# Two MLPs behind a linear attention on one core: the first batch's queries projected once and woven among the keys

## The chip, the cores and the metric

The kernel runs on one core of one Trainium2 chip. The metric is the time of one execution on the device in microseconds (us). The core has a matrix engine (TensorE, in the profile PE, with its weight loads as PEld), VectorE (DVE), ScalarE (ACT), GpSimd (POOL), and SyncE (SP), which here only issues transfers. Transfers are issued by SP, ACT and POOL, each in its own order.

## The reference

Random-feature attention on 4 batches of 8 heads with 576 tokens and 64 columns per head, then two MLPs on the 2304 tokens:

```python
def phi(x):
    proj = np.einsum('bhsd,df->bhsf', x, w_phi)               # 128 features
    proj = proj - np.max(np.abs(proj), axis=-1, keepdims=True)
    return np.concatenate([np.exp(proj), np.exp(-proj)], axis=-1)
q_p, k_p = phi(q), phi(k)
kv  = np.einsum('bhsf,bhsd->bhfd', k_p, v)
z   = np.sum(k_p, axis=2)
num = np.einsum('bhsf,bhfd->bhsd', q_p, kv)
den = np.einsum('bhsf,bhf->bhs', q_p, z)[..., None] + 1e-06
x   = (num / den).transpose(0, 2, 1, 3).reshape(2304, 512)
h = x @ w_in;   x = np.maximum(0.01 * h, h) @ w_out           # 512 -> 2048 -> 512
g = x @ w_gate; out = (g * (1 / (1 + np.exp(-g))) * (x @ w_val)) @ w_out2   # 512 -> 1536 -> 512
```

The subtracted maximum is one number per token and head; for a query it makes the same factor in `num` and `den`, apart from the 1e-06.

## The kernel before

Heads go in pairs (j = 0 to 3), because two heads of 64 columns fill the 128 partitions. Tokens go in five blocks of 96 or 128 for the keys and in two halves of 288 (t = 0, 1) for the queries. Batches are done one after another. While TensorE works on the MLPs of one batch, the attention of the next lies between their steps. Only the first batch has nothing to lie beside: its attention is the start of the program, and the change is there.

**First batch, keys.** `first_k` projects two blocks (L446, two heads of 128 features at once), takes the largest absolute value per token and head (L459), subtracts it (L60) and makes both exponentials on ACT (L464, L465). `first_back` multiplies them with the values, beside which stand columns of ones for `z` (L220), and `k_z` copies the sum of all blocks to SBUF (`kvh`).

**First batch, queries.** `first_q` projects the queries of two blocks with tokens on partitions, only to take the maxima (L473). `q_m` turns these maxima and spreads them over 18 groups of 32 tokens with a mask (L330, L333, L335). `q_exp` then projects the queries a second time, now with features on partitions (L393), and adds the negative maxima by a second matmul with `sel` into the same PSUM bank (L394); ACT makes the exponentials (L396, L397). `q_num` multiplies with `kvh` (L414), `q_fin` turns the denominators, inverts, turns them back and multiplies (L422 to L432), and splits the result in a high and a low part, `xh` (ACT, L63) and `xl` (DVE, L60). The MLP's matmuls take these as their moving side.

The later batches have another way for the queries: `q_p` projects them once with features on partitions, and a reduction that turns as it goes (L352) takes maxima over 32 partitions out of PSUM; `q_m_t` turns what is left on TensorE (L364), ends the maximum (L369) and spreads it (L372 to L377). `q_exp` adds the `sel` matmul to the projection that is still in its bank.

`pm` and `pa` are two pools of four PSUM banks each. `first_k`, the query projections and the MLP products use `pm`, `q_num` and the key sums use `pa` (`bk`).

**Weights.** They arrive as 64-bit numbers; `w_to_f32` makes them 32-bit (ACT L595, L596, L599; DVE L600 or L604 and L605, L610) and `w_split` splits them in high and low parts (L620, L60). Some results are stored (`kept`, `parts`) and read back by later batches. In the first attention, `early` converts the first four gate weights and stores them; they are read back before the gate's first unit.

**What sets the order.** `first_steps` makes a list of steps: in each come the next key block pair, the products of the pair two steps back, and the query maxima of the pair four steps back; sixteen steps of `q_exp` and, two behind, `q_num` and `q_fin` follow. The tile framework then puts the instructions of each engine in an order by a model of their times and priorities; within that order every engine waits for its operands by semaphores. The rows of that order below are from the built programs.

Of the kernel before, what the change touches and what calls it, by code (L numbers as in the profile page):

```python
# [17 lines left out]
P = 128  # L18
B, H, S, D = 4, 8, 576, 64
F = 128  # L20
# [12 lines left out]
NC = TOPS + P + 18 + NB  # L33
# [9 lines left out]
def linear_attention_two_mlps(ctx: ExitStack, tc, qT, kT, vt, w_phi, w1, w2, wg, wv, w3, cst, out):  # L43
# [25 lines left out]
    mask = cst_sb[:, TOPS + P : TOPS + P + 18]  # L69
    mask_t = cst_sb[:, TOPS + P + 18 : NC]  # L70
    sel = const.tile([P, 4, P], F32R, name="sel")
# [6 lines left out]
    mm = [const.tile([P, 32], F32R, name=f"mm{i}") for i in range(4)]  # L78
# [3 lines left out]
    def load_constants():  # L82
        signs.append(T([P, 4, P], F32, "es", 5))
# [41 lines left out]
    def lean(b):  # L125

        return b >= 1
# [198 lines left out]
    def q_m(b, j):  # L326
        n = 2 * NST
        m = mq.pop((b, j))
        t = mm[j % 2]
        dve.tensor_copy(t[:, 0:n], m)  # L330
        sub(t[:, n : 2 * n], m, t[:, 0:n].bitcast(F32))
        mt = T([P, 32], F32, "mt", 1)
        dve.transpose(out=mt, in_=t.bitcast(F32))  # L333
        r = mrow[b, j] = T([P, 18, 32], F32R, "acc", 4)
        dve.tensor_tensor(  # L335
            out=r,
            in0=mt.rearrange("p (o i) -> p o i", o=1).to_broadcast([P, 18, 32]),
            in1=mask.rearrange("p (k o) -> p k o", o=1).to_broadcast([P, 18, 32]),
            op=ALU.mult,
        )  # L340

    def q_p(b, j, t):
# [18 lines left out]
    def q_m_t(b, j, t):  # L361
# [8 lines left out]
        x = mm[2 + t]  # L370
# [3 lines left out]
        if t == 0:  # L374
            mrow[b, j] = T([P, 2 * NB, 32], F32R, "mrow", 1)
# [4 lines left out]
            in1=mask_t.rearrange("p (k o) -> p k o", o=1).to_broadcast([P, NB, 32]),  # L380
# [3 lines left out]
    def q_exp(b, j, h, t):  # L384
        if lean(b):
            ps = pt.pop((b, j, h, t))[:, 0:HT]
            r = mrow[b, j][:, NB * t : NB * t + NB].rearrange("p k i -> p (k i)")
            pe.matmul(ps, sel[:, 2 + h], r, start=False, stop=True, skip_group_check=True)  # L388
        else:
            ps = bk(b)[:, 0:HT]  # L390
            c = slice(HT * t, HT * t + HT)
            r = mrow[b, j].rearrange("p k i -> p (k i)")[:, c]
            pe.matmul(ps, wbd[:, h], raw["q", b, j][:, c], start=True, stop=False)  # L393
            pe.matmul(ps, sel[:, h], r, start=False, stop=True)  # L394
        f = T([P, 2, HT], F32, "ff" if lean(b) else ("ff", "fh", "fl")[(2 * t + h + j) % 3], 3)
# [46 lines left out]
    def project(kind, j, s, n):  # L442
        ps = bk(0)
        for i in range(n):
# [3 lines left out]
                raw[kind, 0, j][:, o],  # L448
# [5 lines left out]
        return ps[:, 0 : 2 * F * n].rearrange("p (r f) -> p r f", f=F)  # L454

    def first_k(j, s, n):
        pv = project("k", j, s, n)
# [11 lines left out]
    def first_q(j, s, n):  # L469
        pv = project("q", j, s, n)  # L470
        if s == 0:
            mq[0, j] = T([P, 2 * NST], F32, "mq", 2)
        dve.tensor_reduce(  # L473
            out=mq[0, j][:, 2 * s : 2 * s + 2 * n], in_=pv, axis=AX.X, op=ALU.max, apply_absolute_value=True
        )
        if s + n == NST:
            q_m(0, j)

# [6 lines left out]
    def first_steps():  # L485

        n, lag = len(pairs), 4
        steps = [[] for _ in range(n + lag)]
# [4 lines left out]
        groups = [(j, t, h) for j in range(NP) for t in range(2) for h in range(2)]  # L493
        for i in range(len(groups) + 2):
            todo = []
            if i < len(groups):
                j, t, h = groups[i]
                todo.append(lambda j=j, t=t, h=h: q_exp(0, j, h, t))
            if i >= 2:
                j, t, h = groups[i - 2]  # L500
                todo.append(lambda j=j, t=t, h=h: q_num(0, j, h, t))
                if h == 1:
                    todo.append(lambda j=j, t=t: q_fin(0, j, t))
            steps.append(todo)
# [169 lines left out]

    def early(key):

        w_load(key, "gp", 5)
        w_to_f32(key)
        del wf[key]

# [421 lines left out]

    def splits(i):
        for k in slots[i]:
            ahead(loaded, w_load, done[0] + 2)
            ahead(conv, w_to_f32, done[0] + 2)
# [133 lines left out]
```

## Time and profile before

| | |
|---|---|
| Time, median of three runs | 1075.07 us (1073.3 to 1075.19) |
| Profiled execution | 1074.16 us, span 1072.3 us |
| TensorE busy | 1050.2 us, 98% of the span |
| DVE busy | 793.6 us, 74% |
| ACT busy | 651.0 us, 61% |
| Transfers | 237.37 MB, mean 221 GB/s |

Busy time is the time in which an engine has at least one instruction running; matmuls overlap each other, so a row's mean time is more than its place in the sequence costs. In the profile a matmul of 32-bit numbers appears as two pieces. The shares are means over stages that differ: the first batch's attention, the MLPs of batches 0 to 2 with the next batch's attention between, and the last batch.

### The profile page before, as it was taken

Reading aid. Unit: us, or ns where it says so; the run is one execution under the profiler, and the core shown is the slowest. Engines: PE = TensorE matmul, PEld = TensorE weight load, DVE = VectorE, ACT = ScalarE, POOL = GpSimd, SP = SyncE. Lnnn points to the kernel's source line nnn. Section 1 sums busy time; section 2 is a strip of 40 time slices with the busy share of each in tenths; the row PEclk is TensorE's granted clock in tenths of the full one; section 3 lists DMA queues with packets and bytes.
Section 4 is the critical chain, followed back from the end, with each engine's and each line's share of the span. In section 5 each row is a group of like instructions: output and inputs, shape, how many; then the busy total and the mean of one; then the engine's idle time right before and its main releaser. Section 6 shows DMA issues by size and latency. Waiting matters only on the chain.

```text
span 1072.3 us, 20451 instructions
## 1 busy us (share of the span) xinstructions
PE 1050.2 (98%) x7670; PEld 1025.1 (96%) x7670; DVE 793.6 (74%) x1712; ACT 651.0 (61%) x1443; POOL 21.9 (2%) x57
## 2 busy tenths in 40 slices
PE   9989999999999999999999989999999999999998
PEld 8869999999999999999999989999999999999998
DVE  5987788888889978879685855958879632468473
ACT  4878887789868787656553466745444334336542
POOL 1000100000000000000000000000000000000000
PEclk9999999999999999999999999999999999999999
DMA  9536767557665995686553386436977767658542
GB/s 301 172 101 221 247 197 264 189 194 236 213 217 187 332 356 195 258 335 225 180 184 131 120 331 224 176 126 235 326 261 263 275 216 276 203 176 293 192 144 84
DMA packets 101922, 237.37 MB, mean 221 GB/s; under 512 B 19904, under 2 KB 35648, under 8 KB 101824
## 3 DMA queue, kind: packets, MB, share of 16 engines
q1 hardware_dynamic: 95136, 220.73, 59.6%
q0 software_dynamic: 4032, 14.68, 3.6%
q8 instruction: 61, 1.00, 0.4%
q10 hardware_dynamic: 2656, 0.66, 0.3%
q14 instruction: 37, 0.30, 0.1%
HBM read 170.49 MB, written 65.54 MB: 220 GB/s over the span
## 4 chain that ended last, share of the span: by engine, by line
PE 64%; DMA 5%; ACT 2%; DVE 2%; issue 0%; SPq 0%; DVEq 0%; ACTq 0%
PE pm L691 44%; PE pa L817 9%; PE pm L817 5%; PE pa L414 2%; PE pa L232 2%; DMA wr<-kept 1%; PE pa L179 1%; DMA wi<-parts 1%; DMA parts<-wi 1%; DMA wi<-in_wv_dram 1%; DMA sums<-wr 1%; DMA vhl<-parts 0%; PE pa L388 0%; PE pa L350 0%; DVE xl L60 0%
## 5 line engine op out<-in xcount | busy, mean ns | idle before, releaser
L691 PE MATMUL pm<-xh,wi 128*128 128x288 f32 x1664 | 352.7, 298 | 2.1 <-ACT xh L63 0.9
L691 PE MATMUL pm<-gp,wo 128*128 128x288 f32 x2256 | 339.0, 296 | 2.6 <-ACT acc L63 1.3
L691 PEld LDWEIGHTS pm<-gp,wo 128*128 128x128 f32 x2256 | 312.0, 188 | 4.9 <-ACT gp L63 2.0
L691 PEld LDWEIGHTS pm<-xh,wi 128*128 128x128 f32 x1664 | 272.2, 188 | 6.0 <-ACT xh L63 1.7
L691 PE MATMUL pm<-xl,wi 128*128 128x288 f32 x832 | 246.5, 297 | 0.5 <-DVE xl L60 0.5
L691 PEld LDWEIGHTS pm<-xl,wi 128*128 128x128 f32 x832 | 156.3, 188 | 1.6 <-DVE xl L60 1.2
L758 DVE TENSOR_TENSOR acc<-pm,acc 128x288 f32<-128x288 f32 x160 | 70.1, 452 | 43.9 <-PE pm L691 43.3
L60 DVE TENSOR_TENSOR gp<-es,gp 128x576 fp32r<-128x576 f32 x94 | 70.5, 750 | 28.5 <-ACT gp L63 28.0
L63 ACT ACTIVATE gp<-es 128x576 fp32r<-128x576 f32 x94 | 64.4, 687 | 28.7 <-DVE es L739 23.4
L60 DVE TENSOR_TENSOR wi<-wr,wi 128x512 fp32r<-128x512 f32 x96 | 65.2, 684 | 20.6 <-ACT wi L620 19.8
L620 ACT ACTIVATE wi<-wr 128x512 fp32r<-128x512 f32 x96 | 59.8, 634 | 29.0 <-PE pm L691 8.2
L817 PE MATMUL pm<-xh,wi 128*128 128x288 f32 x272 | 62.6, 296 | 2.4 <-DMA wi<-parts 1.5
L60 DVE TENSOR_TENSOR fl<-ff,fh 128x512 fp32r<-128x512 f32 (+1 forms) x72 | 51.2, 713 | 9.2 <-ACT fh L63 8.8
L596 ACT ACTIVATE wi<-wi 128x512 int32<-128x512 uint32 x64 | 43.6, 682 | 23.5 <-DMA wi<-in_w_dram 16.5
L595 ACT ACTIVATE wr<-wi 128x512 f32<-128x512 f32 x64 | 43.8, 684 | 10.9 <-DMA wi<-in_w_dram 6.8
L817 PEld LDWEIGHTS pm<-xh,wi 128*128 128x128 f32 x272 | 46.4, 188 | 3.6 <-DVE es L863 2.0
L610 DVE TENSOR_TENSOR wr<-wr,wi 128x512 uint16<-128x512 uint16 x64 | 48.1, 752 | 0.9
L63 ACT ACTIVATE fh<-ff 128x512 fp32r<-128x512 f32 (+1 forms) x72 | 47.3, 663 | 1.0
L417 ACT ACTIVATE dn<-pa 64x288 f32<-64x288 f32 x64 | 26.1, 407 | 30.1 <-PE pa L414 29.2
L719 ACT ACTIVATE es<-pm 128x288 f32<-128x288 f32 x72 | 29.3, 420 | 22.3 <-PE pm L817 17.1
L63 ACT ACTIVATE acc<-pm 128x288 f32<-128x288 f32 x64 | 26.3, 424 | 26.0 <-PE pm L691 25.9
L739 DVE SCALAR_TENSOR_TENSOR es<-pm,es 128x288 f32<-128x288 f32 x72 | 32.1, 449 | 12.6 <-PE pm L691 12.3
(217 smaller groups left out, 2086.8 us busy)
## 6 DMA issues: line engine op xcount, KB each, us to landing
wo<-parts SPq DMA_DIRECT2D x77, 512.0 KB, 6.1
wi<-parts SPq DMA_DIRECT2D x68, 512.0 KB, 6.0
parts<-wi SPq DMA_DIRECT2D x56, 512.0 KB, 4.6
wi<-in_w_dram SPq DMA_DIRECT2D x44, 512.0 KB, 4.6
wr<-kept SPq DMA_DIRECT2D x68, 256.0 KB, 4.4
parts<-wo POOLq DMA_DIRECT2D x28, 512.0 KB, 5.6
kept<-wr SPq DMA_DIRECT2D x40, 256.0 KB, 4.3
wi<-in_wv_dram SPq DMA_DIRECT2D x12, 512.0 KB, 4.1
```

The source lines that it names most:

```text
L60: dve.tensor_tensor(out=o, in0=a, in1=b, op=ALU.subtract)
L63: act.activation(o, a, AF.Copy)
L417: act.activation(dn[b, j, t][D * h : D * h + D], ps[D:P], AF.Copy, bias=1e-6)
L595: act.activation(t, high.bitcast(F32), AF.Abs, scale=REBIAS)
L596: act.activation(low, low.bitcast(U32), AF.Copy, scale=2.0**-29)
L610: dve.tensor_tensor(out=t16, in0=t16, in1=e16, op=ALU.add)
L620: i = act.activation(t[:, 0], r, AF.Copy)
L691: m = pe.matmul(ps, w, x[:, c], start=(i == 0), stop=(i == n - 1))
L719: act.activation(o, i, AF.Prelu, alpha=0.01)
L739: dve.scalar_tensor_tensor(out=g[:, c], in0=ps, scalar=0.5, in1=g[:, c], op0=ALU.mult, op1=ALU.mult)
L758: dve.tensor_tensor(out=acc[o][:, t], in0=ps, in1=acc[o][:, t], op=ALU.add)
L817: m = pe.matmul(ps, a, b, start=start and n == 0, stop=stop and n == 5, skip_group_check=True)
```

## The change

The queries of the first batch go the way of the later batches: one projection with features on partitions, here in plain 32-bit (`wbd`), maxima turned from PSUM, `sel` added in the same bank. `first_q`, `q_m` and the constants for them are gone. `first_steps` now gives every call a time and sorts by it, so that the queries of a pair stand among the keys of the next. The early conversions of four gate weights are gone; those weights are converted in their turn like the others. The warm-up has five matmuls for three. `wbd` is loaded from ACT's queue, and the first keys come in two transfers. The splits of the first four weights are no longer called in one step but in four.

```diff
-        for i in range(3):
+        for i in range(5):
             pe.matmul(ps[:, 0 : 2 * F], zero[:, 0:F], zero, start=True, stop=True)
...
-        nc.sync.dma_start(out=t, in_=kT[b, j])
-        if not (b or j):
-            nc.sync.dma_start(out=wbd.rearrange("p h f -> p (h f)"), in_=w_phi)
+        if b or j:
+            nc.sync.dma_start(out=t, in_=kT[b, j])
+        else:
+            nc.scalar.dma_start(out=wbd.rearrange("p h f -> p (h f)"), in_=w_phi)
+            for c in (slice(0, 256), slice(256, S)):
+                nc.sync.dma_start(out=t[:, c], in_=kT[b, j][:, c])
...
-            a = qs[b, j][h][:, c]
-            pe.matmul(ps, wst_h, a, start=True, stop=False)
-            pe.matmul(ps, wst_l, a, start=False, stop=True)
+            if b == 0:
+                pe.matmul(ps, wbd[:, h], raw["q", b, j][:, c], start=True, stop=True)
+            else:
+                a = qs[b, j][h][:, c]
+                pe.matmul(ps, wst_h, a, start=True, stop=False)
+                pe.matmul(ps, wst_l, a, start=False, stop=True)
...
-        if lean(b):
-            ps = pt.pop((b, j, h, t))[:, 0:HT]
-            r = mrow[b, j][:, NB * t : NB * t + NB].rearrange("p k i -> p (k i)")
-            pe.matmul(ps, sel[:, 2 + h], r, start=False, stop=True, skip_group_check=True)
-        else:
-            ps = bk(b)[:, 0:HT]
-            c = slice(HT * t, HT * t + HT)
-            r = mrow[b, j].rearrange("p k i -> p (k i)")[:, c]
-            pe.matmul(ps, wbd[:, h], raw["q", b, j][:, c], start=True, stop=False)
-            pe.matmul(ps, sel[:, h], r, start=False, stop=True)
+        ps = pt.pop((b, j, h, t))[:, 0:HT]
+        r = mrow[b, j][:, NB * t : NB * t + NB].rearrange("p k i -> p (k i)")
+        pe.matmul(ps, sel[:, h], r, start=False, stop=True, skip_group_check=True)
...
-        for i, p in enumerate(pairs):
-            steps[i].append(lambda p=p: first_k(*p))
-            steps[i + 2].append(lambda p=p: first_back(*p))
-            steps[i + lag].append(lambda p=p: first_q(*p))
...
+        for i, (j, s, n) in enumerate(pairs):
+            at(i, first_k, j, s, n)
+            at(i + 2.5, first_back, j, s, n)
+        for g in range(2 * NP):
+            j, t = divmod(g, 2)
+            base = 3 + 1.25 * g
+            last = max(base + 2.4, 3 * j + 4.6 + 0.4 * t)
+            at(base + 0.1, q_p, 0, j, t)
+            at(base + 0.9, q_m_t, 0, j, t)
+            for h in range(2):
+                at(base + 1.5 + 0.2 * h, q_exp, 0, j, h, t)
+                at(last + 0.2 * h, q_num, 0, j, h, t)
+            at(last + 0.25, q_fin, 0, j, t)
...
-    pre, made, start = 4, 0, 8
     for i, todo in enumerate(steps):
...
-            splits(-1)
-        if i == 14:
+        if i in (6, 8, 10, 12):
+            split_next()
+        if i == 13:
             split_constants()
             load_k(1, 0)
-        while made < pre * min(1, max(0, (i + 1 - start) / (len(steps) - start))):
-            with tc.high_priority(offset=-300):
-                early(("g", 0, made))
-            made += 1
```

In the rows of order a name is a tile with its number, result first, then operands; a line number belongs to its own kernel. TensorE at the start of the program: `pm` are the PSUM banks of the projections, `raw_87` the keys of the first pair, `pk_110` (before) and `pk_111` (now) its queries. In the kernel before:

```order
L109 MATMUL pm_83<-es_81 128x256 x3
L446 MATMUL pm_141<-wbd,raw_87 128x256 x2
L446 MATMUL pm_150<-wbd,raw_87 128x256 x2
L446 MATMUL pm_168<-wbd,raw_87 128x256
L446 MATMUL pm_184<-wbd,raw_99 128x256 x2
L446 MATMUL pm_193<-wbd,pk_110 128x256 x2
L220 MATMUL pa_159<-xh_90,wo_146 128x128 x8
L446 MATMUL pm_204<-wbd,raw_99 128x256 x2
```

The same place on TensorE in the changed kernel:

```order
L108 MATMUL pm_81<-es_79 128x256 x5
L424 MATMUL pm_142<-wbd,raw_87 128x256 x2
L424 MATMUL pm_151<-wbd,raw_87 128x256 x2
L424 MATMUL pm_160<-wbd,raw_87 128x256
L424 MATMUL pm_181<-wbd,raw_100 128x256 x2
L332 MATMUL pm_190<-pk_111,wbd 128x288
L218 MATMUL pa_168<-xh_91,wo_147 128x128 x8
L332 MATMUL pm_193<-pk_111,wbd 128x288
```

The block projections of the queries (`pm_193<-wbd,pk_110`, 256 columns) are gone, and the 288-column projections that stood in `q_exp` (L393) have come to the front, between the keys (L332).

DVE at the first pair's query maxima (`mq`, now `cst_sb` and `top`) up to the spread maxima `acc` that the `sel` matmul takes. In the kernel before:

```order
L473 TENSOR_REDUCE mq_196<-pm_310 128x2
L330 CAST mm_77<-mq_196 128x10
L60 TENSOR_TENSOR mm_77<-mq_196,mm_77 128x10
L333 STREAM_TRANSPOSE mt_315<-mm_77 128x32
L335 TENSOR_TENSOR acc_317<-mt_315,cst_sb 128x576
L604 TENSOR_SCALAR wr_246<-wr_246 128x512
```

The same place on DVE in the changed kernel:

```order
L354 TENSOR_REDUCE top_205<-pm_193 18x32
L337 TENSOR_REDUCE cst_sb<-pm_220 128x9
L357 CAST mm_77<-top_205 18x32
L337 TENSOR_REDUCE cst_sb<-pm_223 128x9
L60 TENSOR_TENSOR mm_77<-top_205,mm_77 18x32
L362 TENSOR_TENSOR acc_209<-mm_77,cst_sb 128x288
L354 TENSOR_REDUCE top_249<-pm_223 18x32
L357 CAST mm_78<-top_249 18x32
L60 TENSOR_TENSOR mm_78<-top_249,mm_78 18x32
L362 TENSOR_TENSOR acc_209<-mm_78,cst_sb 128x288
L572 TENSOR_SCALAR wr_355<-wr_355 128x512
```

Where one chain of five rows ended in one product of 576 columns, two chains, one per half, lie in each other, with two further maxima (`pm_220`, `pm_223`) between them, and each `top` waits for a turn on TensorE.

TensorE at the end of the attention, where the last numerators (`pa`) meet the first MLP matmuls (`wi`). In the kernel before:

```order
L691 MATMUL pm_823<-xl_643,wi_262 128x288
L691 MATMUL pm_823<-xh_642,wi_262 128x288
L691 MATMUL pm_892<-xl_643,wi_281 128x288
L691 MATMUL pm_892<-xh_642,wi_281 128x288
L414 MATMUL pa_760<-ff_725,kvh_480 128x288 x2
L414 MATMUL pa_771<-fh_736,kvh_480 128x288 x2
L691 MATMUL pm_809<-xh_708,wi_262 128x288
```

The same place on TensorE in the changed kernel, up to the first MLP matmuls:

```order
L349 MATMUL pm_641<-cst_sb 128x128
L372 MATMUL pm_561<-acc_618,sel 128x288
L372 MATMUL pm_564<-acc_618,sel 128x288
L392 MATMUL pa_702<-ff_656,kvh_700 128x288 x2
L652 MATMUL pm_764<-xh_287,wi_371 128x288
L652 MATMUL pm_764<-xl_288,wi_371 128x288
L652 MATMUL pm_764<-xh_287,wi_371 128x288
L652 MATMUL pm_764<-xh_443,wi_371 128x288
```

Before, the last four numerator groups and those ahead of them stood between the MLP's matmuls of the third pair; now the first MLP matmul (`pm_764<-xh_287`) stands behind nearly all of the attention, and only the last pair's work is between the units.

## Rows read from the trace of the kernel before

**Rows 1.** Stretches: length, busy us (instructions) PE, PEld, DVE, ACT, POOL, clock, DMA.
```profile
7.26:22.80 15.54, 15.54 (x100) 14.32 (x100) 10.69 (x26) 9.00 (x18) 0.00 (x0) 1.00 1.10 347
22.80:50.00 27.20, 26.44 (x162) 22.97 (x161) 25.92 (x60) 19.95 (x41) 0.96 (x3) 1.00 0.61 202
...
22.80:84.45 61.65, 55.71 (x292) 45.02 (x290) 54.06 (x126) 45.55 (x103) 2.26 (x6) 1.00 0.44 145
...
170.00:220.00 50.00, 48.95 (x361) 47.82 (x360) 42.24 (x85) 33.78 (x66) 2.22 (x4) 1.00 0.59 191
220.00:310.00 90.00, 86.39 (x601) 81.76 (x600) 81.09 (x172) 80.79 (x164) 4.27 (x8) 1.00 0.70 232
```

**Rows 2.** Timeline (start us, length us, instruction, idle before): DVE's maxima; the last wait.
```profile
22.05 0.76 DVE L335 TENSOR_TENSOR acc<-mt,cst_sb 128x576 fp32r<-128x576 f32 x1
...
84.00 0.45 DVE L60 TENSOR_TENSOR xl<-xf,xh 128x288 fp32r<-128x288 f32 x1
...
84.51 0.40 PE L691 MATMUL pm<-xl,wi 128*128 128x288 f32 x1 [0.37 <-DVE xl L60]
```

**Rows 3.** Timeline of TensorE: warm-up, keys, values, numerators.
```profile
1.10 2.93 PE L109 MATMUL pm<-es 128*128 128x256 f32 x6 [1.10 <-POOL es L106]
...
5.18 6.00 PE L446 MATMUL pm<-wbd,raw 128*128 128x256 f32 x14 [1.15 <-DMA wbd<-in_w_phi_dram]
...
20.73 1.95 PE L220 MATMUL pa<-xh,wo 96*128 96x128 f32 x16
...
25.14 2.75 PE L446 MATMUL pm<-wbd,pk 128*128 128x256 f32 x12
...
50.62 1.13 PE L414 MATMUL pa<-fl,kvh 128*128 128x288 f32 x4
...
52.20 1.13 PE L414 MATMUL pa<-ff,kvh 128*128 128x288 f32 x4
```

**Rows 4.** Groups on DVE, 0 to 100 us: shapes, count, busy us, mean ns, idle before.
```profile
L473 DVE TENSOR_REDUCE mq<-pm 128x4 f32<-128x512 f32 x8 | 5.5, 684 | 0.9 <-PE pm L446 0.9
...
L335 DVE TENSOR_TENSOR acc<-mt,cst_sb 128x576 fp32r<-128x576 f32 x4 | 3.0, 755 | 0.1
L610 DVE TENSOR_TENSOR wr<-wr,gp 128x512 uint16<-128x512 uint16 x4 | 3.0, 743 | 0.1
L600 DVE SCALAR_TENSOR_TENSOR wr<-wr,gp 128x512 int32<-128x512 int32 x4 | 2.8, 693 | 2.6 <-ACT gp L599 2.6
...
L473 DVE TENSOR_REDUCE mq<-pm 128x2 f32<-128x256 f32 x4 | 1.7, 424 | 2.5 <-PE pm L446 2.5
...
L333 DVE STREAM_TRANSPOSE mt<-mm 128x32 f32<-128x32 f32 x4 | 0.8, 208 | 0.1
```

**Rows 5.** Groups on DVE over the whole span: the later batches' query maxima.
```profile
L352 DVE TRANSPOSE_TENSOR_REDUCE cst_sb<-pa 128x9 f32<-128x288 f32 x48 | 22.0, 471 | 5.3 <-PE pa L351 5.2
...
L377 DVE TENSOR_TENSOR mrow<-mm,cst_sb 128x288 fp32r<-128x288 f32 x24 | 10.7, 447 | 0.3
...
L369 DVE TENSOR_REDUCE top<-pa 18x32 f32<-18x128 f32 x24 | 6.5, 270 | 1.6 <-PE pa L364 1.5
...
L372 DVE CAST mm<-top 18x32 fp32r<-18x32 f32 x24 | 3.7, 156 | 0.2
```

**Rows 6.** Groups on ACT, 0 to 100 us: the early conversions.
```profile
L595 ACT ACTIVATE wr<-gp 128x512 f32<-128x512 f32 x4 | 2.8, 701 | 0.0
L599 ACT ACTIVATE gp<-gp 128x512 int32<-128x512 f32 x4 | 2.7, 675 | 0.0
...
L596 ACT ACTIVATE gp<-gp 128x512 int32<-128x512 uint32 x4 | 2.4, 657 | 0.0
```

**Rows 7.** Groups on TensorE over the whole span: the later batches' turn.
```profile
L364 PE MATMUL pa<-cst_sb 128*128 128x128 f32 x24 | 6.6, 274 | 0.5 <-DVE cst_sb L352 0.5
```

**Rows 8.** The chain that ended last: start us, length us, what.
```profile
307.70 8.60 PE pm L691 x65
```

**Rows 9.** The turning maxima of L352: what they waited for (us, times).
```profile
  PE pa L351: 5.2, 5
```

More of the change, by code (lines that the diff above doesn't have):

```diff
@@ L32 @@
 TOPS = 4 * NB
-NC = TOPS + P + 18 + NB
+NC = TOPS + P + NB
 OFF = (0, 128, 256, 352, 448)
@@ L68, in linear_attention_two_mlps @@
     ident = cst_sb[:, TOPS : TOPS + P]
-    mask = cst_sb[:, TOPS + P : TOPS + P + 18]
-    mask_t = cst_sb[:, TOPS + P + 18 : NC]
-    sel = const.tile([P, 4, P], F32R, name="sel")
+    mask = cst_sb[:, TOPS + P : NC]
+    sel = const.tile([P, 2, P], F32R, name="sel")
     ones = const.tile([P, P], F32R, name="ones")
@@ L77, in linear_attention_two_mlps @@
     wbd_l = const.tile([P, 2, F], F32R, name="wbd_l")
-    mm = [const.tile([P, 32], F32R, name=f"mm{i}") for i in range(4)]
+    mm = [const.tile([P, 32], F32R, name=f"mm{i}") for i in range(2)]
     signs = []
     def load_constants():
-        signs.append(T([P, 4, P], F32, "es", 5))
+        signs.append(T([P, 2, P], F32, "es", 5))
         nc.sync.dma_start(out=cst_sb, in_=cst[:, 0:NC])
@@ L324, in q_split @@
         sub(s1[0:D], r[D:P], s1[D:P].bitcast(F32))
[L326 to L340, printed above, removed]
     def q_p(b, j, t):
@@ L369, in q_m_t @@
         dve.tensor_reduce(out=top, in_=turned.rearrange("r (g i) -> r i g", g=4), axis=AX.X, op=ALU.max)
-        x = mm[2 + t]
+        x = mm[t]
         hi = x[0 : 2 * NB]
@@ L379, in q_m_t @@
             in0=x.bitcast(F32).rearrange("p (o i) -> p o i", o=1).to_broadcast([P, NB, 32]),
-            in1=mask_t.rearrange("p (k o) -> p k o", o=1).to_broadcast([P, NB, 32]),
+            in1=mask.rearrange("p (k o) -> p k o", o=1).to_broadcast([P, NB, 32]),
             op=ALU.mult,
@@ L447, in project @@
                 ps[:, 2 * F * i : 2 * F * i + 2 * F],
-                raw[kind, 0, j][:, o],
+                raw["k", 0, j][:, o],
                 wbd.rearrange("p h f -> p (h f)"),
@@ L467, in first_k @@
             ff[0, j, s + i] = f[:, i]
[L469 to L477, printed above, removed]
     def first_back(j, s, n):
@@ L485, in first_steps, with at @@
     def first_steps():
-        n, lag = len(pairs), 4
-        steps = [[] for _ in range(n + lag)]
-        for i, p in enumerate(pairs):
-            steps[i].append(lambda p=p: first_k(*p))
-            steps[i + 2].append(lambda p=p: first_back(*p))
-            steps[i + lag].append(lambda p=p: first_q(*p))
[L493 to L504, printed above, removed]
+        events = []
+        def at(time, fn, *args):
+            events.append((time, len(events), lambda: fn(*args)))
+        for i, (j, s, n) in enumerate(pairs):
[11 more added lines that the diff above has]
+            at(last + 0.25, q_fin, 0, j, t)
+        steps = [[] for _ in range(int(max(e[0] for e in events)) + 1)]
+        for time, _, fn in sorted(events, key=lambda e: e[:2]):
+            steps[int(time)].append(fn)
         return steps
@@ L673, in w_sums @@
             nc.sync.dma_start(out=d, in_=t)
[L675 to L679, printed above, removed]
     gp, acc, x2h, x2l, sg = ({} for _ in range(5))
@@ L1101, in depth, with split_next @@
         return 4 if any(k[1] == 1 for k in nxt) else 5
+    def split_next():
+        ahead(loaded, w_load, done[0] + 2)
+        ahead(conv, w_to_f32, done[0] + 2)
+        ahead(done, w_split, done[0] + 1)
+        keep_all_but(2 if done[0] < len(order) and order[done[0]][1] < 2 else 0)
+        ahead(loaded, w_load, done[0] + depth())
     def splits(i):
         for k in slots[i]:
-            ahead(loaded, w_load, done[0] + 2)
-            ahead(conv, w_to_f32, done[0] + 2)
-            ahead(done, w_split, done[0] + 1)
-            keep_all_but(2 if done[0] < len(order) and order[done[0]][1] < 2 else 0)
-            ahead(loaded, w_load, done[0] + depth())
+            split_next()
     atts = {}
@@ L1144, in linear_attention_two_mlps @@
             fn()
-        if i == 4:
+        if i == 2:
             query_constants()
@@ L1172, in _constants @@
     import numpy as np
-    c = np.zeros((P, NC + 4 * P), np.float32)
+    c = np.zeros((P, NC + 2 * P), np.float32)
     c[:, TOPS : TOPS + P] = np.eye(P)
-    signs = c[:, NC:].reshape(P, 4, P)
-    blocks = [(s, a) for s in range(NST) for a in range(VAL[s] // 32)]
-    for p in range(P):
-        a, r = divmod(p, 32)
-        if r >= 4 * NST:
-            continue
-        st, h = divmod(r % (2 * NST), 2)
-        signs[p, h] = -1.0
-        for k, (s2, a2) in enumerate(blocks):
-            c[p, TOPS + P + k] = float(s2 == st and a2 == a)
+    signs = c[:, NC:].reshape(P, 2, P)
     for part in (0, 32):
@@ L1188, in _constants @@
             for k in range(NB):
-                c[part + NB * h + k, TOPS + P + 18 + k] = 1.0
-                signs[part + NB * h + k, 2 + h] = -1.0
+                c[part + NB * h + k, TOPS + P + k] = 1.0
+                signs[part + NB * h + k, h] = -1.0
     return c
```

13 lines of the change are left out of this document (5 added, 8 removed).

## The prediction

> **What bounds the kernel now.** I read the stretches first [rows 1]. From 88 us on TensorE hardly stops: even in the weakest later stretch, 220 to 310 us, it is busy 86.39 of 90. The change leaves the sum of that later work alone, so a gain has to come from the time before the first MLP block runs without stops. There DVE carries the load. In 22.80 to 84.45 us it is busy 54.06 of 61.65 us, and in the part to 50 us 25.92 of 27.20 (95%); what is left, 50 to 84.45, has 28.14 of 34.45 (82%). The reader should see in the waits why the end of this stretch is set by DVE [rows 2]: the last row of TensorE that still waits is a matmul at 84.51 us, for the low half `xl` that DVE (L60) starts at 84.00 and ends at 84.45. So the measure of the change is how much earlier that `xl` comes (last pair, first half of the tokens). The profiled execution took 1074.16 us, 1.86 more than its span and 0.9 below the median of the three runs; the sum is made against 1074.16.
>
> **The start.** The warm-up's six pieces end at 4.03 us, TensorE then waits 1.15 us for `wbd`, and fourteen key pieces take 6.00 us, 0.43 each; the same pieces take 2.75/12 = 0.229 at 25 us [rows 3]. [...] Ten pieces at 0.43 to 0.49 last from 1.10 to about 5.7 us and start the last at about 5.0, so that rest is filled. `wbd` now goes first on ACT's queue, ahead of six value loads that each move back by one place, and the first key columns come as a smaller transfer on SP's. Fourteen pieces at 0.229 save 2.8 us of TensorE. DVE idles 4.85 of the 15.54 us up to 22.80, where the first query maxima are spread out (L335 starts at 22.05 and lasts 0.76) [rows 1, 2]; no more than that can go, and if the warm-up itself holds up the first key matmul, 0.5 us is lost. Between -0.5 and 4.85 I take 2 us, near the 2.8, because the new chain for the first maxima has two trips to TensorE in it. That point then lies at 20.8 us.
> [...]
>
> **Queries on DVE.** Removed: eight maxima of 0.684 and four of 0.424 us (7.2), and four times the old spreading (L335 0.755, the turn 0.208, two small casts priced at 0.156 each: 5.1) [rows 4, 5]. Added: sixteen turning maxima of 0.471 (7.5) and eight times 0.270 + 0.156 + 0.156 + 0.447 (8.2); the last three forms are those that later batches use, and the subtraction is priced as the cast [rows 5]. Net, DVE gets 3.4 us more. Each of the eight groups also gains a trip: DVE's maxima, a turn on TensorE, DVE again, then the `sel` matmul; before, only DVE's result was waited for.
>
> **No early conversions.** In this stretch DVE loses four shifts of 0.693 and four additions of 0.743 us: 5.7 [rows 4]. ACT loses four times 0.701 + 0.675 + 0.657 = 8.1 us [rows 6]. So DVE's work behind the start changes by 15.7 - 12.3 - 5.7 = -2.3, from 54.06 to 51.8 us.
>
> **Queries on TensorE.** Twenty projections of two pieces go: 40 x 0.229 = 9.2 us [rows 3]. The sixteen 288-column projections are not new, they stood in `q_exp` and move forward. Added are eight turns, of 0.274 us at most: 2.2 [rows 7]. The attention's own matmuls then are keys 9.2, values 160 pieces x 1.95/16 = 19.5, sixteen groups of projection, `sel` and two numerator matmuls at 52.20 - 50.62 = 1.58 (25.3; both [rows 3]), turns 2.2: 56.2 us. With 42 MLP matmuls of 8.60/65 = 0.132 ahead of the last `xl` (5.5) [rows 8], and a start at 5.2, TensorE alone could be done at 66.9 us. It is not the bound; its 7 us saved count only as far as DVE waits less for it.
>
> **Interleaving.** Before, keys and query maxima came first and the sixteen numerator groups last, where DVE had only the long chain of transposes and products plus conversions, and stood still 6.3 us in 50 to 84.45. Now these chains lie among key work of later pairs. How busy DVE will be is the main unknown: no lower than 54.06/61.65 = 88% if the trips cost what the chain gives back, no higher than 100%. The nearest rows are the mixed stretch to 50 us (95%) and 220 to 310 (81.09/90 = 90%) [rows 1]; I take 93%. Then 51.8/0.93 = 55.7 us, and the `xl` ends at 20.8 + 55.7 = 76.5 us: 7.95 us earlier than 84.45. What TensorE does behind it is the same in both: the two other halves are covered by units that are ready.
>
> **Given back.** The four gate weights are now converted with those of the value matrix, in about 175 to 225 us, where before they were read back ready. In 170 to 220 TensorE loses 1.05 of 50 us (2%), in 220 to 310, where gate and value weights are both converted, 3.61 of 90 (4%) [rows 1]. Two per cent more of 55 us is 1.1 us; ACT there is busy 33.78 of 50, which is the cover. Without it the price is up to ACT's 8.1 us; nothing is the other end, and a gain is excluded, since work is only added. I take 1.2. SP loses four loads of 512 KB and four stores in front of the first batch's next loads, and four reads back; its transfers are not what the first stretch waits for, so they count nothing, up to the start term's own bound.
>
> **Sum.** 1074.16 - 7.95 + 1.2 = 1067.4 us. At 88% (58.9 us, end 79.7) it is 1070.6, at 100% (51.8, end 72.6) 1063.5; with a start 2 us to either side the own range is 1062 to 1072.
>
> **Rivals.** (1) *TensorE and DVE both stay fed.* For: 95% in the first mixed stretch. With DVE at 100% and a start 4.85 us earlier, the end is 17.95 + 51.8 = 69.8, still above TensorE's 66.9; take 71.5. Against: the numerators wait for PSUM that DVE empties. Time 1074.16 - 12.95 + 0.6 = 1061.8, at best 1060.
> (2) *The conversions cost their full price.* ACT's 8.1 us come back later, where the gain has to be paid out: 1074.16 - 7.95 + 8.1 = 1074.3, no change. For: DVE and ACT are at 90% in 220 to 310 us. Against: 16 of 50 us free on ACT in the stretch before.
> (3) *The turned maxima stall DVE: slower.* DVE takes its queue in order, and behind each of the two maxima of a group stand conversions, key maxima and the other chain's transposes. In later batches five of these maxima waited for their projection for 5.2 us together [rows 9]. If all sixteen trips (eight to the projection, eight to the turn) wait 1.04 us, DVE idles 16.6 us, and the end is 20.8 + 51.8 + 16.6 = 89.2: 1074.16 + 4.75 + 1.2 = 1080.1. It decides from 10.6 us of idle time on (83.25 us, where the gain equals the give-back). Against: other rows stand between a maximum and the use of its turn, and in 22.80 to 50 us DVE had PE as its source and idled only 1.3 us.
> [...]
> [...]
>
> **Chances.** Forecast 0.60, (1) 0.15, (2) 0.10, (3) 0.09, (4) 0.06. A measurement of this kernel cannot tell less than about 0.2% (2.1 us) from no change. Faster: the forecast, (1) and (4), 0.81; same: (2), 0.10; slower: (3), 0.09. The range 1061 to 1073.5 leaves out most of (2), (3) and a part of (1).
>
> **What would show it.** Key pieces at 0.23 us well before 10 us, and the first product with `mask` done near 20.8 us; DVE about 93% busy from there; the `xl` of the last pair's first half ending near 76.5 us; TensorE's lost time in 170 to 225 us up by about 1 us; the rest of the span shifted as a block. Wrong if DVE shows waits for L349's turns of a microsecond each, if the `xl` ends after 80 us, or if the shift shrinks by several us between 170 and 310 us.

## The result, and the profile after

The changed kernel took 1084.41 us (median of six runs, 1081.25 to 1087.22) beside 1075.13 us for the kernel before on the same chip: a ratio of 1.0085, 95% interval [1.0062, 1.0108]. It is 9 us slower, where 7 us faster was forecast. The profiled execution took 1085.46 us, its span is 1083.5. In the text, a ratio is always to the kernel before as it ran beside; times worked out from ratios use 1075 us.

First the page of the changed kernel, TensorE's busy time and the granted clock in 40 slices of 27 us:

```profile
PE 1052.4 (97%) x7642; PEld 1025.2 (95%) x7642; DVE 795.2 (73%) x1730; ACT 648.9 (60%) x1443; POOL 21.7 (2%) x57
...
PEclk9699999999999999999999999999999999999999
```

The clock is below 0.9 only in the second slice, in the first attention. The stretches that answer to [rows 1], and behind them two shorter ones:

```profile
7.26:22.80 15.54, 12.44 (x68) 10.33 (x68) 8.84 (x25) 8.87 (x17) 0.32 (x1) 0.89 0.91 263
22.80:50.00 27.20, 18.42 (x79) 14.06 (x79) 25.11 (x61) 17.69 (x39) 0.31 (x1) 0.72 0.57 188
22.80:84.45 61.65, 48.77 (x236) 39.19 (x236) 50.93 (x126) 37.70 (x85) 1.81 (x5) 0.82 0.38 121
170.00:220.00 50.00, 48.30 (x355) 46.84 (x355) 42.33 (x84) 40.59 (x87) 2.63 (x5) 1.00 0.74 262
220.00:310.00 90.00, 87.90 (x614) 83.23 (x613) 81.01 (x172) 77.75 (x159) 4.25 (x8) 1.00 0.65 216
...
11.50:15.00 3.50, 3.50 (x16) 3.28 (x16) 0.66 (x2) 2.08 (x5) 0.00 (x0) 0.57 1.04 287
...
34.00:52.00 18.00, 10.63 (x26) 7.38 (x27) 15.60 (x36) 10.54 (x22) 0.31 (x1) 0.53 0.42 131
```

From 22.80 to 50 us TensorE fell from 26.44 us busy to 18.42, and that at a mean clock of 0.72; DVE is still busy 25.11 of 27.20. The clock is low in four places: 0.57 in 11.50 to 15.00 us, 0.50 from 35 to 52 us, and 0.50 again in 66 to 68 and in 84 to 86 us. Behind 170 us little differs. TensorE's timeline in the changed kernel shows the start, and then the stretch that is lost:

```profile
4.92 3.18 PE L424 MATMUL pm<-wbd,raw 128*128 128x256 f32 x14
...
29.84 1.03 PE L424 MATMUL pm<-wbd,pk 128*128 128x256 f32 x4
...
35.62 2.29 PE L392 MATMUL pa<-ff,kvh 128*128 128x288 f32 x4 [3.04 <-ACT kvh L63]
...
42.96 0.85 PE L372 MATMUL pm<-acc,sel 128*128 128x288 f32 x2 [3.03 <-DVE acc L362]
...
45.94 1.33 PE L392 MATMUL pa<-fh,kvh 128*128 128x288 f32 x2 [2.14 <-ACT fh L374]
47.06 1.91 PE L424 MATMUL pm<-wbd,pk 128*128 128x256 f32 x4
```

The fourteen key pieces take 0.23 us each, as forecast (6.00 us together before, [rows 3]). But then TensorE rests 3.04, 3.03 and 2.14 us within 14 us, and four key pieces that took 1.03 us at 29.84 take 1.91 at 47.06, 1.85 times as long. The granted clock reads 0.50 from 35 us, within the rest of 3.04 us, to 52 us. Why TensorE waits for `acc` is seen on DVE. These are the rows of one group's chain (maxima of the turned product L354, cast L357, the low part L60 `mm`, the spreading L362) and some of those between:

```profile
20.18 0.46 DVE L362 TENSOR_TENSOR acc<-mm,cst_sb 128x288 fp32r<-128x288 f32 x1
...
33.41 0.27 DVE L354 TENSOR_REDUCE top<-pm 18x32 f32<-18x128 f32 x1
...
34.58 0.70 DVE L578 TENSOR_TENSOR wr<-wr,wi 128x512 uint16<-128x512 uint16 x1
35.19 0.40 DVE L572 TENSOR_SCALAR wr<-wr 128x512 int32<-128x512 int32 x1
...
37.05 0.16 DVE L357 CAST mm<-top 18x32 fp32r<-18x32 f32 x1
37.14 0.67 DVE L573 SCALAR_TENSOR_TENSOR wr<-wi,wr 128x512 int32<-128x512 int32 x1
...
40.65 0.18 DVE L60 TENSOR_TENSOR mm<-top,mm 18x32 fp32r<-18x32 f32 x1
...
41.24 0.73 DVE L578 TENSOR_TENSOR wr<-wr,wi 128x512 uint16<-128x512 uint16 x1
...
42.47 0.44 DVE L362 TENSOR_TENSOR acc<-mm,cst_sb 128x288 fp32r<-128x288 f32 x1
...
90.30 0.46 DVE L60 TENSOR_TENSOR xl<-xf,xh 128x288 fp32r<-128x288 f32 x1 [0.64 <-ACT xh L63]
```

Four instructions of 1.05 us together last from 33.41 to 42.91, 9.50 us, because rows of weight conversions (L572, L573, L578), key features and other groups' products stand between them in DVE's queue. This is the longest of the eight chains; the others take 1.2 to 4.8 us, all eight together 28.9. The first spreading ended at 20.64 (20.8 forecast), the first half's `xl` of the last pair at 90.76 (76.5 forecast; 84.45 before, [rows 2]). On ACT the same happens ahead of the `kvh` copy, for which TensorE waited 3.04 us:

```profile
32.00 0.68 ACT L563 ACTIVATE wr<-wi 128x512 f32<-128x512 f32 x1
32.58 0.66 ACT L564 ACTIVATE wi<-wi 128x512 int32<-128x512 uint32 x1
33.73 0.66 ACT L563 ACTIVATE wr<-wi 128x512 f32<-128x512 f32 x1 [0.49 <-DMA wi<-in_w_dram]
34.29 0.66 ACT L564 ACTIVATE wi<-wi 128x512 int32<-128x512 uint32 x1
34.97 0.60 ACT L63 ACTIVATE kvh<-pa 128x512 f32<-128x512 f32 x1
```

A ledger of TensorE sums it up. Its rest is the span less the busy time: 1072.3 - 1050.2 = 22.1 us before, 1083.5 - 1052.4 = 31.1 after; of this 8.5 and 17.3 us lie in the first 100 us. TensorE's own work is 1043.7 us for the new path (measured in the variant without conversions below, which has the same matmuls at a mean clock of 0.998; from profile to profile this figure differs by 2 to 4 us). So after against before: own work -6.5, slow pieces +8.7, rest +9.0. That these make up the 11.2 us between the spans is no test, since the rest is defined by the span. The -6.5 also holds the faster key pieces (-2.8) and the longer warm-up (3.98 us for 2.93), so that about -4.8 is left for the new path itself; and the first two terms carry the uncertainty of the 1043.7.

### The profile page after: what moved, and what is told of

It reads as the page before. It is cut to its first block, busy times and chain, and to the rows that moved or that the text cites. A ratio compares the mean times of both kernels' runs of the same rounds, so it can differ in the third digit from the quotient of the medians.

```text
span 1083.5 us, 20399 instructions
## 1 busy us (share of the span) xinstructions
PE 1052.4 (97%) x7642; PEld 1025.2 (95%) x7642; DVE 795.2 (73%) x1730; ACT 648.9 (60%) x1443; POOL 21.7 (2%) x57
## 4 chain that ended last, share of the span: by engine, by line
PE 61%; DMA 6%; DVE 3%; ACT 2%; issue 1%; SPq 0%; DVEq 0%
PE pm L652 42%; PE pa L778 8%; PE pm L778 4%; PE pa L392 2%; PE pa L230 2%; DMA wi<-parts 1%; DMA wi<-in_w_dram 1%; DMA wr<-kept 1%; PE pa L177 1%; DMA sums<-wr 1%; DMA wi<-in_wg_dram 0%; DMA vhl<-parts 0%; PE pa L372 0%; DVE xl L60 0%; PE pa L271 0%
## 5 line engine op out<-in xcount | busy, mean ns | idle before, releaser
L60 DVE TENSOR_TENSOR gp<-es,gp 128x576 fp32r<-128x576 f32 x94 | 70.4, 749 | 26.1 <-ACT gp L63 25.6
L60 DVE TENSOR_TENSOR wi<-wr,wi 128x512 fp32r<-128x512 f32 x96 | 64.9, 683 | 12.0 <-ACT wi L588 11.3
L563 ACT ACTIVATE wr<-wi 128x512 f32<-128x512 f32 x68 | 46.3, 686 | 22.4 <-DMA wi<-in_w_dram 11.4
L60 DVE TENSOR_TENSOR fl<-ff,fh 128x512 fp32r<-128x512 f32 (+1 forms) x72 | 51.1, 712 | 11.2 <-ACT fh L63 10.8
L564 ACT ACTIVATE wi<-wi 128x512 int32<-128x512 uint32 x68 | 46.8, 688 | 18.2 <-DMA wi<-in_w_dram 12.4
L578 DVE TENSOR_TENSOR wr<-wr,wi 128x512 uint16<-128x512 uint16 x68 | 51.0, 750 | 0.8
L680 ACT ACTIVATE es<-pm 128x288 f32<-128x288 f32 x72 | 29.7, 418 | 27.2 <-PE pm L778 16.6
```

Of the source, the lines that this page charges most:

```text
L60: dve.tensor_tensor(out=o, in0=a, in1=b, op=ALU.subtract)
L563: act.activation(t, high.bitcast(F32), AF.Abs, scale=REBIAS)
L564: act.activation(low, low.bitcast(U32), AF.Copy, scale=2.0**-29)
L578: dve.tensor_tensor(out=t16, in0=t16, in1=e16, op=ALU.add)
L680: act.activation(o, i, AF.Prelu, alpha=0.01)
```

## Experiments

**Is it the clock?**

```diff
+        for _ in range(2 if b == 0 else 0):
+            x = raw["q", b, j][:, HT * t : HT * t + HT]
+            pe.matmul(ps, nil, x, start=False, stop=False, skip_group_check=True)
         r = mrow[b, j][:, NB * t : NB * t + NB].rearrange("p k i -> p (k i)")
         pe.matmul(ps, sel[:, h], r, start=False, stop=True, skip_group_check=True)
```

> The changed kernel, and in each of the sixteen query groups of the first attention two more matmuls of 288 columns against a tile of zeros, which add nothing to the result: some 15.7 us more work for TensorE, none for the other engines. Main theory (TensorE rests 2 to 3 us at a time between the query chains, its granted clock falls to 0.50 and every piece behind it takes twice as long, some 8 us in all): the granted clock between 34 and 52 us reads 0.9 to 1.0, the low half xl of the last pair ends some 3 to 8 us before the changed kernel's 90.76 us, and the time is 1077 to 1082 us. Rival (the clock is only a sign of the rest; VectorE and ScalarE set the pace and TensorE's slow pieces lie in their shade): xl ends at 90 to 92 us whatever the clock, the time is 1084 to 1087. Third (TensorE's added work costs its own price): xl later by 5 to 15 us, 1089 to 1099.

Measured: 1.0089 [1.0067, 1.0110], the changed kernel's ratio again. TensorE's row on the page:

```profile
PE 1059.0 (98%) x7706; PEld 1032.0 (95%) x7706; DVE 796.3 (74%) x1730; ACT 651.0 (60%) x1443; POOL 21.6 (2%) x58
```

In the stretch that was slow the clock came back in part:

```profile
34.00:52.00 18.00, 13.40 (x49) 9.53 (x50) 16.20 (x38) 10.67 (x22) 0.31 (x1) 0.81 0.35 107
```

1059.0 is the own work of 1043.7 and 15.3 more, where the filling was estimated at 15.7: most of the slow pieces' 8.7 us are gone, the mean granted clock is 0.997 after 0.987, and the rest is 24.3 us. Yet the first half's `xl` ends at 91.26 us. The filling took the place of the rest and of the slowness, and nothing of the real work came sooner: the expected 3 to 8 us did not come. We read this as TensorE having been slow, for the most part, where it would otherwise have stood still; it is not shown separately. Whether a part of the 8.7 us could be had stays open, since the filling stands ahead of the `sel` matmuls and can delay each by up to 0.98 us.

**The parts of the change alone.** Deferral in the kernel before (the loop that calls `early` deleted), the same undone in the changed kernel (loop put back), the start in the kernel before (`load_k`'s transfers and `range(5)`), and start and deferral together.

> The kernel before without the four early gate conversions, all else as it was: part of the change alone. Main theory (the loss comes from the interleaved order): the deferral costs 1 to 2 us behind 170 us and the first stretch becomes shorter or stays, so the time lies between 1070 and 1077 us. The prediction's own terms (-5.7/0.93 + 1.2) say 1070. Rival (the deferred conversions are what made the changed kernel slower): 1080 to 1085 us, with the loss showing behind 170 us.

> The changed kernel with the four early gate conversions put back in its first attention. Main theory: they add 8.1 us to ScalarE and 5.7 us to VectorE where both already stand ahead of the query chains, so xl of the last pair ends 2 to 8 us after the changed kernel's 90.76 us, and 1.5 to 2 us come back behind 170 us: 1084 to 1091 us. Rival (deferral is the loss): 1074 to 1078 us. Rival (VectorE had room, it was busy 54.45 of 70.12 us, so the conversions fit in): xl unchanged, 1082.5 to 1083.5 us.

> The kernel before with the start of the changed one alone: five warm-up matmuls, the feature weights on ScalarE's queue, the first keys in two transfers. The prediction's start term: the fourteen first key pieces take 0.23 us each instead of 0.43, the first query maxima are spread out about 2 us earlier than 22.05 us, xl of the last pair ends about 2 us before 84.45, the time is 1072 to 1074 us. Rival (VectorE carries this stretch and the start is given back to it by 84 us): the pieces are fast, xl ends at 84 to 85 us, the time is 1074 to 1076 us.

> The kernel before with the start of the changed one and without the four early conversions: both parts, neither the new way to the maxima nor the interleaving. If the parts add up (start -1 to 0, no early conversions -3 to -4 us): 1071 to 1073 us, and against the variant with the queries behind the keys it shows what the new way to the maxima is worth by itself: that one 4 to 7 us less by TensorE's 7 us of work saved, or more than this one if the turned maxima cost. Rival (the start is given back to VectorE): as without the early conversions alone, 1072 to 1074 us.

Measured: 0.9961 [0.9941, 0.9982]; 1.0010 [0.9991, 1.0029]; 0.9994 [0.9977, 1.0011]; 0.9987 [0.9970, 1.0003]. The start gains nothing that can be told (the interval goes from -2.5 to +1.2 us), though its `xl` ends at 81.60, 2.85 us sooner. Without early conversions the kernel before gains 4.2 us; yet putting them back gives the changed kernel 8.1 us, against the main theory. Its `xl` stays late (87.40). The two parts together gain 1.4, not the sum of 4.8. No part alone is slower in the kernel before; and the new path and order without the deferral are not slower either (1.0010). The loss needs the new path or order and the deferral together.

**Is it the interleaving?** The query groups behind the keys, as before:

```diff
-            base = 3 + 1.25 * g
-            last = max(base + 2.4, 3 * j + 4.6 + 0.4 * t)
+            base = 12 + 1.25 * g
+            last = base + 2.4
```

> The changed kernel with one edit: its query groups (projection, turned maxima, exponentials, numerators) are issued behind the twelve key steps, in the order of the kernel before, and no longer between them. Main theory (the interleaved order is what costs; the new way to the maxima is sound): TensorE's own work stays some 7 us less than before, its clock stays at 1.00 to 60 us, its rest in the first 100 us is like that of the kernel before (8.5 us) or less; 1064 to 1071 us. Rival (3) of the prediction (the turned maxima themselves stall VectorE and TensorE, wherever they stand): rests of 1 to 3 us ahead of each sel matmul, now in a row, 1076 to 1088 us.

Measured: 1.0146 [1.0126, 1.0167], 15.7 us slower than before: the main theory fell here. TensorE's timeline of this variant:

```profile
52.81 0.27 PE L349 MATMUL pm<-cst_sb 128*128 128x128 f32 x1
56.04 0.33 PE L349 MATMUL pm<-cst_sb 128*128 128x128 f32 x1 [2.95 <-DVE cst_sb L337]
60.07 1.55 PE L372 MATMUL pm<-acc,sel 128*128 128x288 f32 x4 [3.70 <-DVE acc L362]
61.42 2.12 PE L392 MATMUL pa<-fh,kvh 128*128 128x288 f32 x4
```

The rows repeat for each pair, some 13.5 us apart (the `sel` rows stand at 60.07, 73.61 and 87.13): the turn waits for the maxima, `sel` waits for the spreading, and nothing else is there for TensorE. A projection stays in its bank from `q_p` until the exponentials have read it, and a group holds two of the four `pm` banks (`bk(0)`). The kernel before projected twice, and the maxima released their bank at once: its four spreadings start at 22.05, 39.07, 47.59 and 48.62 us, its sixteen `sel` matmuls from 42.78 to 63.07, and none of them waits.

**Is it the conversions ahead?** In each of the two kernels, the first nine weights take one GpSimd copy of their high words in place of the conversion, so that the weights are not the true ones and only the times are read. The nine are not the same: in the kernel before four of them are the early gate weights.

```diff
+        raws.append(key)
+        if len(raws) <= 9:
+            pool.tensor_copy(out=t, in_=high.bitcast(F32))
+            wf[key] = t
...
+            return
```

> The changed kernel without the conversion of the first nine weights: ScalarE's two and VectorE's three instructions on each are left out, and a GpSimd copy of the high words takes their place, so the weights are not the true ones. That takes 9 x (0.675 + 0.675) = 12.2 us from ScalarE and 9 x (0.736 + 0.677 + 0.402) = 16.3 us from VectorE in 20 to 100 us. Main theory (conversions that stand in the two in-order queues ahead of the query chains make TensorE rest): no rest above 1 us ahead of L372's and L392's matmuls between 30 and 50 us, the clock 0.9 to 1.0 there, the last xl of the first attention (95.19 to 95.65 us) 10 to 16 us earlier, 1067 to 1074 us. Rival (the trips between TensorE and VectorE of the interleaved chains are too long by themselves): rests and lower clock remain, xl at most 5 us earlier, 1078 to 1083 us.

> The control to the variant without conversions: the kernel before, its first nine weight conversions (the four early ones among them) replaced by a GpSimd copy of the high words, so the weights are not the true ones. If the conversions are a burden to both orders alike, it gains as much as the changed kernel does without them. Main theory (they hurt the interleaved order more): it gains 4 to 8 us, 1067 to 1072 us, less than the changed kernel's 10 to 16. Rival: the same gain as there or more, so that a difference of about 9 us remains between the two.

Measured: 0.9918 [0.9898, 0.9937] and 0.9887 [0.9867, 0.9907]. The changed kernel gains 18.0 us, the kernel before 12.1; the 9.1 us between them shrink to 3.3. The chain of the changed kernel without conversions, on DVE:

```profile
33.52 0.27 DVE L354 TENSOR_REDUCE top<-pm 18x32 f32<-18x128 f32 x1
33.72 0.46 DVE L337 TRANSPOSE_TENSOR_REDUCE cst_sb<-pm 128x9 f32<-128x288 f32 x1
34.11 0.13 DVE L357 CAST mm<-top 18x32 fp32r<-18x32 f32 x1
34.27 0.18 DVE L60 TENSOR_TENSOR mm<-top,mm 18x32 fp32r<-18x32 f32 x1
34.49 0.46 DVE L362 TENSOR_TENSOR acc<-mm,cst_sb 128x288 fp32r<-128x288 f32 x1
...
35.00 0.54 PE L372 MATMUL pm<-acc,sel 128*128 128x288 f32 x2 [0.53 <-DVE acc L362]
```

The same four instructions now last 1.43 us instead of 9.5; all eight chains together take 18.0 us instead of 28.9. TensorE waits 0.53 us for `acc` in place of 3.03 (the row is TensorE's), and its clock reads 1.00 from 34 to 52 us. So the conversions are much of what stretches the chains; but they are in both kernels, and only in the changed one does TensorE wait at their end.

**Is it the held projection?** Projecting twice again, first in the order with the keys ahead (maxima along with the keys), then interleaved with two steps more for the exponentials, then interleaved at the changed kernel's own steps, and last the slack without the second projection. The first hunk below is in the first three, the two others in the second and the last; the first has a list of times of its own besides, with the groups' exponentials two steps apart, so it differs from the variant above in more than the projection:

```diff
-        ps = pt.pop((b, j, h, t))[:, 0:HT]
+        if b == 0:
+            pt.pop((b, j, h, t))
+            ps = bk(b)[:, 0:HT]
+            pe.matmul(ps, wbd[:, h], raw["q", b, j][:, HT * t : HT * t + HT], start=True, stop=True)
+        else:
+            ps = pt.pop((b, j, h, t))[:, 0:HT]
...
-            last = max(base + 2.4, 3 * j + 4.6 + 0.4 * t)
+            last = max(base + 2.4, 3 * j + 4.6 + 0.4 * t) + 2
...
-                at(base + 1.5 + 0.2 * h, q_exp, 0, j, h, t)
+                at(base + 3.5 + 0.2 * h, q_exp, 0, j, h, t)
```

> The changed kernel with the queries projected twice again: the turned maxima are taken along with the keys, as early as before, and release their PSUM bank; the exponentials' projection is made anew behind the keys (sixteen groups of 0.49 us more for TensorE, 7.8 us). It differs from the variant with the queries behind the keys only in this. New theory (the projections that are held in PSUM tie the maxima, the turn, the spreading and the exponentials into one chain that TensorE waits for, and the second projection of the kernel before bought the slack): no rests ahead of the sel matmuls behind 50 us, TensorE's clock stays at 1.00 there, 1072 to 1079 us, against 1090. Rival (the turned path is long and heavy for VectorE wherever it stands): 1083 to 1095 us, with rests ahead of the turns or the sel matmuls.

> As the one with two projections, but the query groups stay interleaved with later pairs' keys as in the changed kernel, with the exponentials and numerators two steps later, so that the maxima have time. 7.8 us more for TensorE than in the changed kernel. If held projections are the fault and the interleaving is harmless: 1073 to 1080 us, the clock above 0.9 in 34 to 52 us. If the interleaving itself is at fault (conversions, key maxima and transposes between the query rows of VectorE): 1083 to 1092 us, with rests of 2 us and more for acc, kvh and the exponentials as in the changed kernel.

> The variant with two projections in the interleaved order, but with the exponentials and numerators at the changed kernel's own steps (no two steps more): the second projection alone, 7.8 us more for TensorE. If the held PSUM banks are the fault: 1074 to 1079 us, as with the two steps. If the slack of two steps did it: 1084 to 1091 us, with rests ahead of the exponentials' matmuls between 30 and 50 us, the clock low there.

> The changed kernel with its one projection held in PSUM, and the exponentials and numerators two steps later: the slack alone, no work more for TensorE. If the slack is what counts: 1068 to 1076 us (7.8 us of TensorE's work less than with two projections), the clock above 0.9 in 34 to 52 us. If the held banks are the fault, a longer hold of two of the four banks does not help or makes it worse: 1083 to 1095 us, with rests as in the changed kernel.

Measured: 1.0025 [1.0008, 1.0041]; 0.9998 [0.9976, 1.0020]; 1.0001 [0.9979, 1.0022]; 1.0025 [1.0008, 1.0043]. With 7.8 us more of work for TensorE, the order with the keys ahead gains 13.0 us and the interleaved one 9.0, the whole loss. Slack alone, with the projection held, gains 6.5 of the 9.1: a longer hold did not harm, so a mere want of banks is not the cause, and the time lies between the ranges expected for either theory. The stretch 20 to 60 us, of the changed kernel and then of the one with two projections at the same steps (columns as in [rows 1]):

```profile
20.00:60.00 40.00, 30.48 (x147) 24.51 (x148) 34.69 (x84) 25.92 (x57) 0.52 (x2) 0.79 0.46 150
```
```profile
20.00:60.00 40.00, 36.14 (x189) 29.50 (x188) 38.27 (x96) 30.19 (x66) 1.15 (x4) 0.96 0.44 137
```

With two projections DVE is busy 38.27 of 40 us (96%) instead of 34.69, ACT 30.19 instead of 25.92. The chains are no shorter: all eight take 33.1 us with two projections and 28.9 in the changed kernel. But TensorE's rest in the first 100 us falls from 17.3 to 6.2. We read it so: TensorE can go on with keys and other projections, and these keep the other two fed. The framework makes a new order for each variant, and no run holds that order fixed, so this step is argued and not shown. What TensorE waited for from 20 to 100 us, with two projections, and then with the held one and slack:

```profile
PE pm L377 <- DVE acc L362: 2.6, 2, 2.2
PE pa L397 <- ACT fl L379: 0.9, 2, 0.6
PE pm L332 <- ACT ff L380: 0.7, 1, 0.7
```
```profile
PE pm L372 <- DVE acc L362: 4.2, 4, 1.2
PE pm L332 <- DVE wo L60: 3.5, 2, 2.8
PE pa L392 <- ACT fl L374: 2.8, 2, 2.4
```

The waits of the projections (L332) for `wo` are waits for a bank: L332 does not read `wo`, but DVE's reading of key products (L60) frees one. Such waits are a price of the hold where it is longest. In the changed kernel itself no L332 waits in the first 100 us; there TensorE waits for `acc`, for `kvh` and for the exponentials instead.

**Do the early conversions pay here?** The loop of the kernel before, put into the variant with two projections at the changed kernel's steps and into the one with hold and slack:

> The variant with two projections at the changed kernel's steps (which ran like the kernel before), with the four early gate conversions put back. If the deferred conversions had a price of their own (the reading of the 7 us that putting them back gave the changed kernel): 1066 to 1070 us. If those 7 us came from where the waits of the held chain fell, and conversions in the first attention cost as in the kernel before (where leaving them out gave 3 to 4 us): 1074 to 1080 us.

> The held projection with two steps more of slack (1.0025 times the kernel before) and the early gate conversions put back. If deferral has its own price: 1070 to 1074 us. If not, and the conversions only burden VectorE and ScalarE in the first attention: 1078 to 1084 us.

Measured: 0.9949 [0.9931, 0.9967] and 0.9981 [0.9965, 0.9997]: 5.6 and 4.7 us gained. The first, 1070.85 us (median), has the lowest ratio of all versions that do the whole computation; it lies below the kernel before and the changed one, by 5.5 and about 14.6 us, but cannot be told from the kernel before without early conversions (0.9961). Four of the versions make a table: with the projection held 1.0085 without and 1.0010 with early conversions, with two projections 1.0001 and 0.9949. So the hold costs 9.0 and 6.6 us and the deferral 8.1 and 5.6, and the changed kernel is the one cell that has both; either alone leaves it level with the kernel before. (The two prices of each part agree within the intervals.) TensorE's waits of 170 to 310 us, without and with the early conversions (two projections):

```profile
PE pm L657 <- DVE wi L60: 1.2, 2, 1.0
PE pm L657 <- ACT es L685: 0.9, 1, 0.9
PE pm L657 <- DVE acc L724: 0.8, 3, 0.5
PE pm L657 <- ACT acc L63: 0.8, 1, 0.8
```
```profile
PE pm L663 <- DVE acc L730: 1.1, 2, 0.7
PE pa L377 <- DVE mrow L362: 0.4, 1, 0.4
PE pm L663 <- DVE gp L60: 0.4, 1, 0.4
```

The waits for weights (`wi`) go, and TensorE's rest in 170 to 310 us falls from 5.3 to 2.0. In the kernel before it is 4.7 us with the early conversions and without. Why they do not pay in that order is open.

## Why the prediction was wrong

- **What bounds the kernel.** Where it looked was right: the loss lies before 100 us. Its measure was not: that the time moves as the last pair's first `xl` does. With the start alone `xl` came 2.85 us sooner and with two projections 5.9 us (78.53), and neither gained; with two projections and early conversions it came 0.8 us sooner (83.64) and 5.5 us were gained. TensorE's ledger (own work, slow pieces, rest) says at least in which term the time lies.
- **The start.** 20.64 us for 20.8, pieces of 0.23 us: right, and (4), in which the start gains nothing (1069.4 us) because the pieces stay slow, wrong about the pieces. But the clock did not stay at 1.00: it reads 0.57 in 11.50 to 15.00 us, behind a rest of 1.63 us. That a filled rest makes the pieces fast was the author's estimate; no run shows it by itself, nor the 2 us taken for the start. With the whole new start in the kernel before, the fourteen pieces took 3.75 us (0.27 each), the first spreading started at 20.55 us, 1.50 sooner, and the worth of 2 us did not show (0.9994), though the interval does not exclude it. The pieces of the kernel before sped up about 5.6 us after their start, from 0.43 us apart to 0.22, while the granted clock read 1.00 throughout.
- **Queries on DVE and TensorE.** The durations held: in the first attention L337 takes 0.473 us, L354 0.264, L362 0.448. TensorE's own work fell by 6.5 us, of which about 4.8 belong to the 7.0 forecast here; the difference is within what this figure varies from profile to profile.
- **Interleaving: the step that failed.** "I take 93%" for DVE, and no lower than 88%, "if the trips cost what the chain gives back". It was busy 50.93 of 61.65 us in the old stretch (83%), and 54.45 of 70.12 (78%) from the first spreading to the `xl`; TensorE was busy 48.77 of the 61.65. With two projections DVE had 96% from 20 to 60 us, but 51.11 of 57.89 (88%) from 20.64 us to its `xl`; with the early conversions besides it had 58.30 of 63.00 (93%). What was left out is that the removed projections were not only 9.2 us of work: they released the banks at once, and with them back at the changed kernel's own steps the 9.0 us are gone (1.0001). The working even took for an advantage that "other rows stand between a maximum and the use of its turn"; those rows made 9.5 us out of 1.05 in the worst chain.
- **The clock** was looked at for the start alone. Its falls from 11 us on were not foreseen; they added about 8.7 us to TensorE's busy time, though filling the rests earned nothing. The longest, 0.50 from 35 to 52 us, began within the rest of 3.04 us for ACT's copy of `kvh`.
- **Given back: the second step that failed.** Forecast 1.2 us, against 5.7 us of DVE's work (6.1 at 93%) that the first stretch was to lose: 4.9 us gained by the deferral. Putting the conversions back gained 4.7 to 8.1 us in three pairs of runs with the new path, of which 2.4 to 3.3 us is TensorE's rest in 170 to 310 us. So in the changed kernel the deferral cost 8.1 us where 4.9 were to be gained, 13 of the 17 us between forecast and measurement. (The hold's 6.6 to 9.0 us overlap with this; the two are not a sum.) What of it lies outside TensorE's rest is not explained. In the kernel before, the deferral did gain (4.2 us).
- **Rivals.** (3) had the right side and the right place, at a chance of 0.09. Its mechanism was half right: from the first spreading to the `xl` DVE idled 15.67 us of the 16.6 priced, but hardly for turns (L354 1.8 us and L337 3.5 us in the first 100 us; the most went to denominators from ACT, 6.4 us); the waiter that counted was TensorE, for `acc` (5.4 us), `kvh` (3.0) and exponentials (4.5). Its price of 4.75 us at the `xl` was 6.3. (2), the deferral at the full price of 8.1 us, came near in price (4.7 to 8.1 with the new path) and gave a part.

## What to carry to other kernels

A second computation of the same product can be what keeps two engines apart: before it is removed, count how long its result will then be held, which buffers that takes, and what the producing engine can do meanwhile. Price a chain in an engine's queue by what stands between its rows (here 9.50 us from the first to the last) and not by the rows (1.05). When a change has several parts, try them crossed: here the hold and the deferral each left the time level, and only both together cost. And measure a change by the busiest engine's work, slowness and rest over the whole span, not by one landmark.

## What the runs showed of the hardware

The granted clock of TensorE was 0.50 from 35 to 52 us of the changed kernel, from within a rest of 3.04 us on, and fell three times more in the first 100 us, the first time to 0.57 in 11.50 to 15.00 us behind a rest of 1.63 us. That a kernel which before read 1.00 in every stretch can lose it in its first attention, for 17 us on end, was not expected. Nor was it that a clock largely brought back by some 15.3 us of work with zeros (0.997 on the mean, 0.81 in 34 to 52 us) left the time where it was.
